# One loader operation per slot of two attention steps, in place of a whole weight in one slot

## Chip, core and metric

The kernel runs on one core of a Trainium2 chip. The metric is the device time of one execution in microseconds (us); the median of three runs of the kernel before is 1209.4 us (1208.53 to 1209.43).

## What is computed

Attention with a learned position bias over 4 batches, 8 heads, 576 positions and 64 columns, then two feed-forward layers on its 2304 x 512 result. Cut to what matters:

```python
scores = scale * q @ k.T + bias          # (4, 8, 576, 576)
attn = softmax(scores); x = attn @ v     # -> x of 2304 x 512
h = x @ w_in;  x = (h * clip(h + 3, 0, 6) / 6) @ w_out
x = (sigmoid(x @ w_gate) * (x @ w_val)) @ w_out2
```

## The kernel before

Three stages follow each other on one core: the bias (to about 61 us of the profile), the attention (61 to 345 us) and the feed-forward layers (the rest). The change touches the attention.

**Steps and slots.** Two heads (a pair) of one batch are 9 steps: 8 steps of 128 query rows of one head, and a ninth for the 64 rows left of both. There are 16 such pairs `n`, so 144 steps, and line 525 walks them in 76 slots of two steps. One slot gives TensorE the scores of its two steps (L262, into a ring of two PSUM tiles `s`), VectorE the sum with the bias and the row minimum (`u`, L266), ScalarE the exponential with its row sum (L282), and for the slot before it the transposes of the probabilities (L320, L328, L335) through a ring of three PSUM tiles `tr`, which ScalarE and VectorE copy out (L310, L312). The products with `v` (L352, L355) collect in one PSUM tile `av`, read by L359. Row sums become reciprocals in L288 and L289, which ScalarE spreads (L293) for a transpose (L299). Since two pairs are 18 steps, nine slots are the period of this work; slots 0, 9, 18, 27, ... begin one.

**Preparation of the next pair.** ScalarE rounds `q` (L230) and GpSimd does the rest of it for `q` and `k` (L234, L238): operations of over 1 us, in rows of several.

**The loader.** Weights come as float32 and are split into a high and a low part for TensorE. For one weight tile that is one DMA on SP's queue (L127, ring of two `raw`), one ScalarE operation (L133), four VectorE operations (L134, L141, L143, L145), one ScalarE rounding into the weight's `slot` (L151) and one GpSimd subtraction (L152). Ten weights are loaded in the attention: line 533 calls `whole()` in slots 12, 18, 24, ... 66. In the last slots line 537 (`tick`, slots 70 and 73) starts the next weights.

**What sets the order.** A scheduler places the instructions of all engines ahead of time, by data and buffers and by the order in which the code is written; on the chip each engine runs its list in that order. `tc.issue_after(x)` keeps the instructions that are traced under it, on the engine of `x` alone, behind `x`.

Of the kernel before, what the change touches and what calls it, by code (L numbers as in the profile page):

```python
# [14 lines left out]
ALU = mybir.AluOpType  # L15
# [28 lines left out]
NPRE = 10  # L44
EVERY = 6
# [50 lines left out]
def block_kernel(ctx: ExitStack, tc: tile.TileContext, q, k, v, mlp, w_in, w_out, w_gate, w_val, w_out2, dist_d,  # L96
                 rows_d, out):
    nc = tc.nc
# [13 lines left out]
    class Loader:  # L112
# [20 lines left out]
                nc.scalar.activation(z, self.raw[i][:, :, 1].bitcast(F32), AF.Abs)  # L133
                nc.vector.tensor_scalar(out=z, in0=z, scalar1=2.0**-15, scalar2=None, op0=ALU.max)  # L134

        def assemble(self, i):
            if i not in self.z:
                return
            raw, z = self.raw.pop(i), self.z[i]
            zi = z.bitcast(I32)  # L140
            nc.vector.tensor_scalar(out=zi, in0=zi, scalar1=3, scalar2=0x3FFFFFF8, op0=ALU.logical_shift_left,  # L141
                                    op1=ALU.bitwise_and)
            nc.vector.scalar_tensor_tensor(out=zi, in0=raw[:, :, 1], scalar=-0x40000000, in1=zi,  # L143
                                           op0=ALU.bitwise_and, op1=ALU.bitwise_or)
            nc.vector.scalar_tensor_tensor(out=zi, in0=raw[:, :, 0], scalar=29, in1=zi,  # L145
                                           op0=ALU.logical_shift_right, op1=ALU.bitwise_or)

        def split(self, i, eng=nc.vector):
            if i in self.z:
# [2 lines left out]
                eng.tensor_tensor(out=slot[:, 1], in0=z, in1=slot[:, 0].bitcast(F32), op=ALU.subtract)  # L152
                self.done = i + 1

        def whole(self):
            i = self.n
            for stage in (self.dma, self.magnitude, self.assemble):
                stage(i)
            self.split(i, nc.gpsimd)
            self.n += 1  # L160

        def tick(self):
            i = self.n
# [11 lines left out]
    def ring(name):  # L175

        if name == "z":
            return stg.tile([P, 512], F32, name="z", bufs=4)
        return stg.tile([P, 2, 512], F32, name="raw", bufs=2)

    load = Loader([w[f] for f in range(NF) for w in (w_in, w_out)]
                  + [w[e] for e in range(NE) for w in (w_gate, w_val, w_out2)])
# [66 lines left out]
    pts, us, avs, last_u = {}, {}, {}, [None]  # L249
# [113 lines left out]
    last_v = [None]  # L363
# [3 lines left out]
    for n in range(NU):  # L367
        i = (NSTEP * n + 5) // 2 + 2
# [8 lines left out]
    def slot_of_two(i):  # L377

        for t in steps(i):
            scores(t)  # L380
            n, s = seq[t]
            p, b = divmod(n, B)
            if s == 0:
                last_v[0] = load_v(n)
            if b == B - 1 and p + 1 < NPAIR and (s % 2 == 1 or s == 8):
                load_bias(p + 1, s // 2)
        for n, a, g in AV.get(i, ()):
            av(n, a, g)
            if g == 4:
                av_out(n, a)  # L390
        for t in steps(i):
            expo(t)
        for t in steps(i - 1):
            n, s = seq[t]
            if s in (5, 8):
                invert(n, s // 6 * 3, s // 6 * 2 + 3)
        for t in steps(i - 2):
            n, s = seq[t]
            if s in (5, 8):
                turn_inv(n, s // 6 * 3, s // 6 * 2 + 3)  # L400
        for t in steps(i - 1):
            trans(t)
            n, s = seq[t]
            if s in REM:
                trans_rem(n, REM[s])
        for t in steps(i):
            if t in PREP:
                n, h = PREP[t]
                prep(n, h)
            for k, (n, h) in PREP.items():  # L410
                if h == 1 and n + 1 < NU and t == k + 3:
                    load_qk(n + 1)
# [6 lines left out]
    with ExitStack():  # L419
# [24 lines left out]
        for r in (slice(NEAR, ND), slice(0, NEAR)):  # L444
# [3 lines left out]
                                op1=ALU.mult)  # L448
# [7 lines left out]
        for ct in range(4):  # L456
# [3 lines left out]
                                    op0=ALU.mult)  # L460
# [15 lines left out]
        for G in range(S // 16):  # L476
            hid = [hids[(4 * G + ct) % 12] for ct in range(4)]
            for ct in range(4):
# [4 lines left out]
                else:  # L483
                    nc.vector.tensor_scalar(out=hid[ct], in0=src, scalar1=bpsi[:, 1, qd : qd + 1], scalar2=None,  # L484
                                            op0=ALU.max)
# [14 lines left out]
        def split_x(x):  # L500
            for c in range(4):
                nc.scalar.copy(XH[:, c], x[c])
                nc.vector.tensor_tensor(out=XL[:, c], in0=x[c], in1=XH[:, c].bitcast(F32), op=ALU.subtract)

        def project(slot, ps=None):
            ps = mp.tile([P, 512], F32, name="h", bufs=4) if ps is None else ps
            for c in range(4):
                wh = slot[:, 0, P * c : P * c + P]
                wl = slot[:, 1, P * c : P * c + P]
                nc.tensor.matmul(ps[:, 0:TW], wh, XH[:, c], start=(c == 0), stop=False)  # L510
                nc.tensor.matmul(ps[:, 0:TW], wl, XH[:, c], start=False, stop=False)  # L511
                nc.tensor.matmul(ps[:, 0:TW], wh, XL[:, c], start=False, stop=(c == 3))  # L512
            return ps[:, 0:TW]

        def hardswish(g, ph):
            nc.scalar.activation(g, ph, AF.Relu, bias=half, scale=1.0 / 6.0)  # L516
            nc.vector.scalar_tensor_tensor(out=g, in0=g, scalar=1.0, in1=ph, op0=ALU.min, op1=ALU.mult)  # L517
            return g
# [5 lines left out]
        for i in range(NSLOT):  # L524
            slot_of_two(i)
            if i == NS // 2:
                w = keep.tile([P, 8 * TW], F32R, name="early").rearrange("p (r c t) -> p r c t", r=2, c=4)
                XH, XL = w[:, 0], w[:, 1]
                split_x([x[:, 0:TW] for x in x1])
            if i in (NS // 2 + 1, NS // 2 + 2):  # L530
                f = len(begun)
                begun[f] = hardswish(ring("z")[:, 0:TW], project(slots[2 * f], pp.tile([P, 2, 512], F32, name="s")[:, 0]))
            if i % EVERY == 0 and i > 10 and load.n < NPRE:
                with tc.issue_after(last_v[0].ins):
                    load.whole()
            if i in PRIME:
                load.tick()

# [156 lines left out]
```

## Time and profile before

| | |
|---|---|
| median of three runs | 1209.4 us |
| profiled execution, its own time | 1207.13 us |
| its span in the trace | 1205.4 us |
| TensorE / VectorE / ScalarE / GpSimd busy | 1187.5 / 682.1 / 574.2 / 133.2 us |
| attention | about 61 to 345 us |

All numbers of the trace belong to the profiled execution; 1.7 us of its time lie around the span. A row of the timeline gives the start, the duration, the engine, the line of the kernel, the operation and its tiles; in square brackets stands idle time ahead of it and who ended it. Matmul ends are modelled, so the distance of two starts says more than a duration. One L352 of the code is two rows of the trace.

### The profile page before, as it was taken

To read this page: it belongs to the slowest core of one execution; us is meant where nothing else is said; L and a number is where in the kernel's file an instruction comes from. 1 tells how busy PE (TensorE), PEld (TensorE's weight loads), DVE (VectorE), ACT (ScalarE), POOL (GpSimd) and SP (SyncE) were. 2 spreads that over 40 slices of the span, in tenths; PEclk is the share of its full clock that TensorE was granted. 3 is DMA by queue.
4 is the path that set the end of the run, shared out by engine and by line. 5 is a ranking of instruction groups with operands and counts; after the bars stand their busy time and mean duration, and the time that the engine had idled before them with its cause. 6 is when DMAs were issued, how large, how long until landed. Compare 5 with 4: busy or idle time off the path is not lost.

```text
span 1205.4 us, 18764 instructions
## 1 busy us (share of the span) xinstructions
PE 1187.5 (99%) x7302; PEld 1057.4 (88%) x7302; DVE 682.1 (57%) x1464; ACT 574.2 (48%) x1224; POOL 133.2 (11%) x108
## 2 busy tenths in 40 slices
PE   8989999999999999999999999999999999999998
PEld 3467777777789999999999999999999999999998
DVE  8967887778876555645565545564431544222332
ACT  7978877877854444434344434333321332221221
POOL 0055545544200000000000000000000000000000
PEclk9999999999999999999999999999999999999999
DMA  6643635353211232212222223322210121101000
GB/s 210 244 141 105 186 100 178 110 164 108 76 53 67 92 105 80 79 62 80 74 69 82 92 88 114 122 80 79 64 58 1 62 79 53 53 1 53 27 27 27
DMA packets 36152, 106.76 MB, mean 89 GB/s; under 512 B 3936, under 2 KB 10336, under 8 KB 36064
## 3 DMA queue, kind: packets, MB, share of 16 engines
q1 hardware_dynamic: 36064, 105.57, 26.9%
q8 instruction: 57, 0.93, 0.3%
q14 instruction: 31, 0.25, 0.1%
HBM read 80.78 MB, written 24.77 MB: 88 GB/s over the span
## 4 chain that ended last, share of the span: by engine, by line
PE 87%; DVE 6%; ACT 3%; DMA 2%; issue 1%; POOL 0%; SPq 0%; DVEq 0%; ACTq 0%
PE o L574 16%; PE h L512 13%; PE h L510 13%; PE h L511 13%; PE o L631 12%; PE s L262 6%; PE av L352 5%; PE tr L320 4%; PE s L489 1%; PE av L355 1%; DVE u L266 1%; DVE x L484 1%; DVE z L143 1%; ACT p L282 1%; PE tr L299 1%
## 5 line engine op out<-in xcount | busy, mean ns | idle before, releaser
L510 PE MATMUL h<-early,slot 128*128 128x384 f32 x952 | 318.9, 335 | 0.0
L512 PE MATMUL h<-early,slot 128*128 128x384 f32 x952 | 318.8, 335 | 0.0
L511 PE MATMUL h<-early,slot 128*128 128x384 f32 x952 | 318.5, 335 | 0.0
L510 PEld LDWEIGHTS h<-early,slot 128*128 128x128 f32 x952 | 178.8, 188 | 2.6
L511 PEld LDWEIGHTS h<-early,slot 128*128 128x128 f32 x952 | 178.7, 188 | 2.5
L512 PEld LDWEIGHTS h<-early,slot 128*128 128x128 f32 x952 | 178.7, 188 | 0.1
L551 ACT CAST gh<-g 128x384 fp32r<-128x384 f32 x166 | 85.0, 512 | 162.4 <-DVE g L646 119.8
L574 PE MATMUL o<-gh,slot 128*128 128x384 f32 x768 | 156.9, 336 | 3.0 <-ACT raw L310 1.8
L646 DVE TENSOR_TENSOR g<-g,h 128x384 f32<-128x384 f32 x72 | 39.8, 553 | 183.1 <-PE h L512 183.1
L574 PEld LDWEIGHTS o<-gh,slot 128*128 128x128 f32 x768 | 134.2, 188 | 6.9 <-ACT raw L310 4.4
L552 DVE TENSOR_TENSOR gl<-g,gh 128x384 fp32r<-128x384 f32 x166 | 92.2, 558 | 79.1 <-ACT gh L551 77.0
L516 ACT ACTIVATE g<-h,half 128x384 f32<-128x384 f32 x94 | 54.5, 580 | 131.1 <-PE h L512 127.5
L262 PE MATMUL s<-k,q 128*128 128x288 f32 x640 | 112.2, 310 | 2.5 <-POOL k L234 1.2
L645 ACT ACTIVATE g<-h 128x384 f32<-128x384 f32 x72 | 35.4, 492 | 165.0 <-PE h L512 165.0
L282 ACT ACTIVATE p<-u,stat 128x576 f32<-128x576 f32 x128 | 98.7, 773 | 28.9 <-DVE stat L266 28.5
L631 PE MATMUL o<-slot,gh 128*128 128x512 f32 x432 | 111.9, 393 | 0.0
L266 DVE CUSTOM_DVE_ANT_0 u<-s,bias 128x576 f32<-128x576 f32 x128 | 93.5, 753 | 24.9 <-PE s L262 24.3
L517 DVE SCALAR_TENSOR_TENSOR g<-g,h 128x384 f32<-128x384 f32 x94 | 51.8, 552 | 95.2 <-ACT g L516 95.1
L262 PEld LDWEIGHTS s<-k,q 128*128 128x128 f32 x640 | 89.0, 189 | 5.9 <-POOL k L234 1.7
L631 PEld LDWEIGHTS o<-slot,gh 128*128 128x128 f32 x432 | 80.1, 188 | 13.6 <-issue 0.2
L574 PE MATMUL o<-gl,slot 128*128 128x384 f32 x384 | 88.5, 334 | 0.0
L352 PE MATMUL av<-ptm,vn 128*64 128x288 f32 x512 | 78.9, 419 | 1.2 <-DVE x L359 0.7
(99 smaller groups left out, 1494.0 us busy)
## 6 DMA issues: line engine op xcount, KB each, us to landing
raw<-in_part_dram SPq DMA_DIRECT2D x68, 512.0 KB, 3.5
nbias<-p SPq DMA_DIRECT2D x18, 576.0 KB, 3.2
early<-in_part_dram SPq DMA_DIRECT2D x32, 288.0 KB, 4.3
bias<-nbias SPq DMA_DIRECT2D x16, 576.0 KB, 6.0
take<-x SPq DMA_DIRECT2D x12, 768.0 KB, 4.1
vn<-in_part_dram SPq DMA_DIRECT2D x16, 320.0 KB, 3.1
early<-in_part_dram SPq DMA_DIRECT2D x16, 304.0 KB, 3.8
part<-raw SPq DMA_DIRECT2D x12, 384.0 KB, 2.6
```

Source lines behind the costliest of these rows:

```text
L262: nc.tensor.matmul(ps[:, a, 0:HS], Q[:, q0 : q0 + P], K[:, r, h, HS * a : HS * a + HS], start=(i == 0), stop=(i == len(mm) - 1))
L266: last_u[0] = nc.vector.tensor_tensor_reduce(out=halves(u), in0=ps[:, :, 0:HS], in1=halves(bt), op0=ALU.add, op1=ALU.min, scale=-0.125, sc ...
L282: nc.scalar.activation(probs(t), us.pop(t), AF.Exp, bias=low[n % 2][:, s : s + 1], scale=-1.0, accum_out=sums[n % 3][:, s : s + 1])
L352: nc.tensor.matmul(ps[64 * h : 64 * h + 64, 0:HS], vt[:, 4 * h + g], ptm[:, h, g, cols], start=(g == 0), stop=False)
L510: nc.tensor.matmul(ps[:, 0:TW], wh, XH[:, c], start=(c == 0), stop=False)
L511: nc.tensor.matmul(ps[:, 0:TW], wl, XH[:, c], start=False, stop=False)
L512: nc.tensor.matmul(ps[:, 0:TW], wh, XL[:, c], start=False, stop=(c == 3))
L516: nc.scalar.activation(g, ph, AF.Relu, bias=half, scale=1.0 / 6.0)
L551: nc.scalar.copy(gh, g)
L552: last_g[0] = nc.vector.tensor_tensor(out=gl, in0=g, in1=gh.bitcast(F32), op=ALU.subtract)
L574: nc.tensor.matmul(os[c][:, 0:TW], sl[:, r, P * c : P * c + P], x, start=(first and r == 0 and x is gh), stop=(last and x is gl))
L631: nc.tensor.matmul(os[i], x[:, P * i : P * i + P], sl[:, r], start=(first and x is gh and r == 0), stop=(end and x is gl))
```

## The change

`whole()` becomes `step(k)`: slot `i` from 6 on does operation `i % 6` of the current weight. 0 is the DMA, 1 is L133 and L134, 2 to 4 are the other three VectorE operations one by one, and 5 is the ScalarE rounding with the GpSimd subtraction. A second `issue_after` keeps the VectorE operation of a slot behind the last `u` of that slot. The first weight starts in slot 6 and the tenth is done in slot 65. No instruction is added or taken away; each engine has the same ones, in another order.

```diff
-        def assemble(self, i):
+        def assemble(self, i, parts=(0, 1, 2)):
...
+            if 0 in parts:
+                nc.vector.tensor_scalar(out=zi, in0=zi, scalar1=3, scalar2=0x3FFFFFF8, op0=ALU.logical_shift_left,
...
-        def whole(self):
+        def step(self, k):
+
             i = self.n
-            for stage in (self.dma, self.magnitude, self.assemble):
-                stage(i)
-            self.split(i, nc.gpsimd)
-            self.n += 1
+            if k == 0:
+                self.dma(i)
+            elif k == 1:
+                self.magnitude(i)
+            elif k < 5:
+                self.assemble(i, (k - 2,))
+            else:
+                self.split(i, nc.gpsimd)
+                self.n += 1
...
-            if i % EVERY == 0 and i > 10 and load.n < NPRE:
-                with tc.issue_after(last_v[0].ins):
-                    load.whole()
+            if i >= EVERY and load.n < NPRE:
+                with tc.issue_after(last_v[0].ins), tc.issue_after(last_u[0].ins):
+                    load.step(i % EVERY)
```

Behind the changed functions the lines of the new kernel are 10 higher: its L276 is L266, its L298 is L288, its L142, L145 and L148 are L141, L143 and L145. The text keeps the old numbers. Three places show how the lists of the engines change; the short read of the accumulator behind each `u` is left out.

VectorE from the last `u` of slot 23 to the first of slot 25, before (`z` and `raw` are the loader's tiles):

```order
L266 ISA u,stat<-s,bias_104 128x576
L134 TENSOR_SCALAR z<-z 128x512
L359 TENSOR_TENSOR x_64<-av,inv 128x288
L312 COPY ptm<-tr 128x4x64
L141 TENSOR_SCALAR z<-z 128x512
L312 COPY ptr<-tr 64x64
L143 SCALAR_TENSOR_TENSOR z<-raw,z 128x512
L312 COPY ptm<-tr 128x4x128
```

and after:

```order
L276 ISA u,stat<-s,bias_104 128x576
L369 TENSOR_TENSOR x_64<-av,inv 128x288
L322 COPY ptm<-tr 128x4x64
L322 COPY ptr<-tr 64x64
L322 COPY ptm<-tr 128x4x128
```

Three loader operations are gone from this slot.

VectorE at the end of a pair, from the first `u` of slot 26 on (the one that reads `bias_m` is the ninth step), before:

```order
L359 TENSOR_TENSOR x_64<-av,inv 128x288
L288 TENSOR_SCALAR stat<-stat 128x6
L289 RECIPROCAL stat<-stat 128x6
L312 COPY ptm<-tr 128x4x128
L266 ISA u,stat<-s,bias_106 128x576
L266 ISA u,stat<-s,bias_m 128x576
L312 COPY ptm<-tr 128x4x128
L266 ISA u,stat<-s,bias_103 128x576
```

and after:

```order
L369 TENSOR_TENSOR x_64<-av,inv 128x288
L134 TENSOR_SCALAR z<-z 128x512
L322 COPY ptm<-tr 128x4x128
L276 ISA u,stat<-s,bias_106 128x576
L298 TENSOR_SCALAR stat<-stat 128x6
L276 ISA u,stat<-s,bias_m 128x576
L299 RECIPROCAL stat<-stat 128x6
L142 TENSOR_SCALAR z<-z 128x512
L322 COPY ptm<-tr 128x4x128
L276 ISA u,stat<-s,bias_103 128x576
```

L288 (new L298) has moved from ahead of both `u` to between them, in slots 17, 26, 35, 44, 53 and 62 alike; in slot 62 a fourth loader operation, L145, stands right behind it, from the weight that line 537 starts. In the slot that follows, 28, the list reads L288, L143, L289 where it read L288, L289, and so also in slots 10, 46 and 64.

TensorE from slot 27 on (`s` scores, `av` products with v), before:

```order
L262 MATMUL s<-k_110,q_108 128x288 x8
L352 MATMUL av<-ptm,vn 64x288 x6
L299 MATMUL tr<-ident,spread 128x128 x3
L320 MATMUL tr<-ident,p 128x128 x4
L328 MATMUL tr<-ident,pm_113 128x64 x4
L262 MATMUL s<-k_110,q_108 128x288 x4
L328 MATMUL tr<-ident,pm_113 128x64 x4
```

and after:

```order
L272 MATMUL s<-k_110,q_108 128x288 x8
L362 MATMUL av<-ptm,vn 64x288
L272 MATMUL s<-k_110,q_108 128x288
L309 MATMUL tr<-ident,spread 128x128 x3
L272 MATMUL s<-k_110,q_108 128x288
L362 MATMUL av<-ptm,vn 64x288 x5
L330 MATMUL tr<-ident,p 128x128 x4
L338 MATMUL tr<-ident,pm_113 128x64 x4
```

A score matmul of the next slot now stands ahead of five of the six products with `v` (slots 27 and 45). On ScalarE the rounding of `q` (L230) has moved there from behind the exponentials of the pair's last two steps to ahead of them, and the copy of `tr` that stood between them stands behind both and behind L293.

## Rows read from the trace of the kernel before

**Rows 1.** The page: busy time and instructions by engine; granted TensorE clock in tenths.

```profile
PE 1187.5 (99%) x7302; PEld 1057.4 (88%) x7302; DVE 682.1 (57%) x1464; ACT 574.2 (48%) x1224; POOL 133.2 (11%) x108
...
PEclk9999999999999999999999999999999999999999
```

**Rows 2.** Windows of nine slots: length, then busy PE, PEld, DVE, ACT, POOL.

```profile
127.15:162.59 35.44, 34.52 (x257) 26.24 (x256) 29.95 (x74) 28.40 (x75) 18.66 (x15) 1.00 0.49 152
162.59:196.78 34.19, 34.19 (x258) 26.23 (x256) 25.86 (x70) 27.67 (x73) 17.21 (x14) 1.00 0.42 120
196.78:232.23 35.45, 34.50 (x258) 26.23 (x256) 29.87 (x74) 28.39 (x75) 18.57 (x15) 1.00 0.47 143
232.23:266.41 34.18, 34.18 (x257) 26.22 (x256) 25.85 (x70) 27.66 (x73) 17.20 (x14) 1.00 0.43 119
```

**Rows 3.** Timeline, VectorE: loader operations of slots 24 and 38.

```profile
149.97 1.19 DVE L134 TENSOR_SCALAR z<-z 128x512 f32<-128x512 f32 x1
...
151.78 0.94 DVE L141 TENSOR_SCALAR z<-z 128x512 int32<-128x512 int32 x1
...
204.62 1.92 DVE L143 SCALAR_TENSOR_TENSOR z<-raw,z 128x512 int32<-128x512 int32 x1
```

**Rows 4.** Timeline, GpSimd, near slots 24 and 35 to 38.

```profile
147.95 2.93 POOL L238 TENSOR_TENSOR q<-early,q 64x640 fp32r<-64x640 f32 x2
150.96 1.48 POOL L238 TENSOR_TENSOR k<-early,k 128x576 fp32r<-128x576 f32 x1
...
195.73 2.25 POOL L234 TENSOR_TENSOR k<-early,one 128x576 fp32r<-128x576 f32 x2 [8.19 <-PE s L262]
197.94 2.79 POOL L238 TENSOR_TENSOR k<-early,k 128x576 fp32r<-128x576 f32 x2
200.80 1.55 POOL L238 TENSOR_TENSOR q<-early,q 64x640 fp32r<-64x640 f32 x1
204.57 1.42 POOL L238 TENSOR_TENSOR q<-early,q 64x576 fp32r<-64x576 f32 x1 [2.22 <-ACT q L230]
```

**Rows 5.** Timeline, TensorE: its waits in slots 24 and 25; slots 36 and 37.

```profile
151.91 0.66 PE L320 MATMUL tr<-ident,p 128*128 128x128 f32 x4 [0.21 <-DVE ptm L312]
...
157.04 0.66 PE L320 MATMUL tr<-ident,p 128*128 128x128 f32 x4 [0.48 <-ACT inv L310]
...
196.78 1.30 PE L262 MATMUL s<-k,q 128*128 128x288 f32 x8
198.00 1.68 PE L352 MATMUL av<-ptm,vn 128*64 128x288 f32 x12
...
201.64 0.46 PE L328 MATMUL tr<-ident,pm 64*128 64x64 f32 x4
```

**Rows 6.** Timeline, VectorE, slots 35 to 37: a pair's end and the next pair's start.

```profile
193.96 0.16 DVE L288 TENSOR_SCALAR stat<-stat 128x6 f32<-128x6 f32 x1
...
194.49 0.69 DVE L312 COPY ptm<-tr 128x512 f32<-128x512 f32 x1
...
195.77 0.08 DVE L266 DVE_READ_ACCUMULATOR2_ANT stat<- 128x1 f32 x1
196.08 0.76 DVE L266 CUSTOM_DVE_ANT_0 u<-s,bias_m 128x576 f32<-128x576 f32 x1 [0.22 <-PE s L262]
...
197.68 0.76 DVE L266 CUSTOM_DVE_ANT_0 u<-s,bias 128x576 f32<-128x576 f32 x1
...
199.04 0.33 DVE L288 TENSOR_SCALAR stat<-stat 128x3 f32<-128x3 f32 x1
...
201.75 0.76 DVE L266 CUSTOM_DVE_ANT_0 u<-s,bias 128x576 f32<-128x576 f32 x1 [2.16 <-PE s L262]
```

**Rows 7.** Timeline, ScalarE: in the bias stage, and in slots 35 to 37.

```profile
30.63 0.78 ACT L482 ACTIVATE x<-x,early 128x576 f32<-128x576 f32 x1 [1.31 <-PE s L489]
...
196.67 0.56 ACT L310 COPY ptm<-tr 128x512 f32<-128x512 f32 x1
...
200.59 0.48 ACT L310 COPY inv<-tr 128x384 f32<-128x384 f32 x1
```

More of the change, by code (lines that the diff above doesn't have):

```diff
@@ L134, in magnitude @@
                 nc.vector.tensor_scalar(out=z, in0=z, scalar1=2.0**-15, scalar2=None, op0=ALU.max)
-        def assemble(self, i):
+        def assemble(self, i, parts=(0, 1, 2)):
             if i not in self.z:
                 return
-            raw, z = self.raw.pop(i), self.z[i]
+            raw, z = self.raw[i], self.z[i]
             zi = z.bitcast(I32)
[L141 to L146, printed above, removed]
+            if 0 in parts:
+                nc.vector.tensor_scalar(out=zi, in0=zi, scalar1=3, scalar2=0x3FFFFFF8, op0=ALU.logical_shift_left,
+                                        op1=ALU.bitwise_and)
+            if 1 in parts:
+                nc.vector.scalar_tensor_tensor(out=zi, in0=raw[:, :, 1], scalar=-0x40000000, in1=zi,
+                                               op0=ALU.bitwise_and, op1=ALU.bitwise_or)
+            if 2 in parts:
+                nc.vector.scalar_tensor_tensor(out=zi, in0=raw[:, :, 0], scalar=29, in1=zi,
+                                               op0=ALU.logical_shift_right, op1=ALU.bitwise_or)
+                self.raw.pop(i)
         def split(self, i, eng=nc.vector):
```

## The prediction

> **What bounds the kernel now.** I read the busy times first: TensorE has 1187.5 of 1205.4 us and the granted clock is full in every slice [rows 1], so the change pays by what it does to TensorE's waits, and the clock is no term. No instruction is added or removed, so only the order in the attention counts. There I read windows of nine slots, the period of the attention's work [rows 2]. They come in two lengths, 34.18 to 34.19 and 35.44 to 35.45 us. The short ones hold one load (slots 30 and 48), the long ones two (18 and 24, 36 and 42). In a short one TensorE is busy to the end, 34.19 of 34.19: this I take as the pace that no reordering beats. A long one has 0.95 less busy time than length.
>
> Then I ask which operation makes a long window long. In slot 24 the loader's L134 takes 1.19 us and its L141 0.94 [rows 3]; shortly behind each a GpSimd operation that was running has ended: the second of two L238 at 150.88 and the next at 152.44 [rows 4]; the loader operation is done some 0.28 us after that. L143 in slot 38 took 1.92 and was done 0.55 after GpSimd's L238 of 204.57. L288 at 199.04 waited in the same way, 0.33 in place of 0.16 [rows 6]. So these VectorE operations stand still until the running GpSimd operation ends. TensorE's waits right behind them are 0.21 on VectorE's copy and 0.48 on ScalarE's [rows 5].
>
> The Trainium skill (SBUF — State Buffer, section "Who interferes with whom") says that the second port pair of VectorE is GpSimd's too, is held for a whole instruction and goes to whoever issues first, and that tensor_scalar and operations with two SBUF inputs ask for it. The trace shows the VectorE half of it, with the times above; no row here shows GpSimd standing behind VectorE.
>
> **What is removed.** Loads in slots 18, 36 and 54 with their partners in 24, 42 and 60 make three long windows, each 35.44 - 34.18 = 1.26 us over the short one. Loads in 30 and 48 cost nothing, since their windows are short, and I take the same for 12 and 66. At best the change gives back 3 x 1.26 = 3.8 us.
>
> **What is added: four terms.** Times are those of slots 35 to 37 [rows 4 to 7], which stand for every pair's end.
>
> (a) A pair's end, six times. L288 ran at 193.96, when GpSimd was idle (8.19 us before 195.73). Now it comes behind the slot's first `u`, at 195.77 + 0.08 = 195.85, and GpSimd has started two L234 at 195.73 that end at about 196.86 and 197.98. So L288 stands until 196.9, and the ninth step's `u` starts there and not at 196.08. It frees the score tile which the second step of the next slot needs: its first matmul comes at about 197.3 (eight from 196.78 on, the next kind at 198.00), the tile is free at 196.9 + 0.76 = 197.7, so TensorE is 0.4 late. In slots 18, 36 and 54 nothing of the loader follows, and part comes back later, because the new order lets TensorE work where it waited ahead of L328 at 201.64. I take 0.3 each, 0.9 in all; bounds 0 and 1.2.
>
> (b) Slots 27 and 45. On top of (a), L141 follows L289 and stands until the second L234 ends: done 197.98 + 0.28 = 198.3; the copy of 0.69 ends at 199.0, and the next `u`, at 197.68 before, starts then and is done at 199.7. TensorE has one product with `v` (0.27) behind its late scores and then a score matmul that needs this `u`: it idles from about 198.5 to 199.7. ScalarE's copy for the other five products, at 196.67 before, comes behind the ninth step's exponential and L293, at about the same 199.6, so no other order of TensorE would save it. 0.4 + 1.2, less the 0.2 that TensorE lost ahead of 198.00 anyway, is 1.4. A part may come back at L328 (1.05 left); if L143 in slot 28, behind L288, misses the gap between two GpSimd operations and stands behind the L238 of 200.80, 0.8 is added to that, 1.85. I take the middle, 1.45, twice: 2.9; bounds 2.1 and 3.7.
>
> (c) Slot 62. L145 of the weight that line 537 starts stands behind L288 ahead of the ninth step's `u`. At 196.9 GpSimd's second L234 runs to 197.98, and as an operation of L143's form it is done 0.55 later, 198.5; that `u` ends at 199.3, and TensorE's second step waits from 197.3: 2.0. L143 in slot 64 can add 1.3. At least it costs what (b) may, 1.05, at most 3.3; I take 2.7, nearer the upper end because L288, L145, L141 and L143 follow each other there into one row of GpSimd operations.
>
> (d) Slots 9 and 10, the first weight. Slot 8 keeps its order, but L141 meets GpSimd (done 198.3), the two `u` end 1.3 us late, L288 stands until the two L238 end at 200.73, and L143 either slips in (L289 done at 201.6) or stands until 200.80 + 1.55 + 0.55 = 202.9 (L289 at 203.1). ScalarE's copy at 200.59 needs it through L293, and TensorE's L328 at 201.64 needs the copy: 0.75 or 2.2 late. I take 1.5, between the two, since the rows do not tell who wins that gap.
>
> **At nothing.** The other loader operations of the new order: a nine-slot window leaves VectorE 34.19 - 25.86 = 8.3 us idle, and in slots 13 to 16, 20 to 24 and 30 to 34 they meet either an idle GpSimd or stand ahead of an L288 that waits for the same GpSimd operation anyway. Without that cover each would cost up to L143's 1.92. The first weight's DMA and L133 move into the bias stage; L133, some 0.7, falls into ScalarE's idle 1.31 ahead of 30.63 [rows 7]; without that cover 0.7, which I add to the upper end. On SP each raw load of weights 1 to 9 stands where that of the weight before stood, so nothing of `q`, `k`, `v` waits longer there.
>
> **Sum.** Added 0.9 + 2.9 + 2.7 + 1.5 = 8.0, removed 3.8: 4.2 us slower. Bounds: 0 + 2.1 + 1.05 + 0.75 - 3.8 = 0.1 and 1.2 + 3.7 + 3.3 + 2.2 + 0.7 - 3.8 = 7.3. The profiled execution took 1207.1 us, 2.3 less than the median; on it the sum gives 1211.3, on the median 1209.4 + 4.2 = 1213.6, and I say 1213.5.
>
> **Rivals.** *It does what it is meant to* (faster): the loader's work hides in every slot, L288 between the two `u` meets no GpSimd operation, and all of 3.8 comes back: 1205.6. The point that decides is 0.12 us wide: L288 at 195.85 against GpSimd's 195.73. Both follow TensorE's scores of the same step, so I see nothing that would open it; for it speaks only that `u` two microseconds late in slot 20 cost little in the old kernel. 0.12.
>
> *The losses cancel the gain*: TensorE takes back part of each delay, L143 slips in each time, and the terms are at their low ends, 3.9 against 3.8: 1209.5. It decides itself in slots 28 and 64, where the trace of before has nothing of the loader. 0.32.
>
> *L143 wins its gap*: VectorE's L143 starts in the gap between two GpSimd operations in slots 10, 28 and 46, and the next GpSimd operation waits for it. Then (b) is at its 2.1 and (d) at its 0.75, with (a) and (c) as taken: 0.9 + 2.1 + 2.7 + 0.75 - 3.8 = 2.65 over, 1212.05. This is about half of my forecast's 0.56, which it moves by 1.5 and not to another sign. The Trainium skill's rule (SBUF — State Buffer, section "Who interferes with whom") that the first to issue holds the pair speaks for it.
>
> *The change doesn't do what it says*: the tie holds VectorE alone, and the lists of ScalarE, GpSimd and TensorE are free. The order shows that the VectorE operations do come one per slot, so this is left only for ScalarE's L133 and L151, which stand next to each other ahead of two exponentials in slots 23, 41 and 59. I count it in the upper end.
>
> **How the numbers follow.** The forecast, slower by 2.5 to 7.3, has 0.56; the cancelled case 0.32; the hidden one 0.12. A measurement of this kernel can tell about 0.2% (2.4 us) from no change, so faster means under 1207.0 and slower over 1211.8: 0.12, 0.32, 0.56. The likeliest case's own range is 1211.8 to 1216.7. The range to hold 8 in 10 leaves out the hidden case and a little above the sum's upper end: 1207.0 to 1216.7.
>
> **What would show it.** In the profile of the changed kernel, the nine-slot windows from slots 18, 36 and 54 should be about 34.5 us and no longer 35.4, those from 27 and 45 about 35.6, the one from 63 over 36, the one from 9 about 35.7. L288 at each pair's end should take 1 us or more, and TensorE should wait for the `u` behind it. If L288 there takes 0.16, (a) to (c) fall and with them the sign. If it does take 1 us but the window from slot 27 stays near 34.2, then TensorE's list absorbs what I booked as loss, and the time is that of the cancelled case or below.

## The result and the profile after

The changed kernel takes 1215.75 us (median of 4 runs, 1215.52 to 1216.55) against 1208.99 us for the kernel before, so the medians are 6.8 us apart. The recorded ratio is 1.0066 (95% interval 1.0053 to 1.0078), which is not the quotient of the medians and would be 8 us; either way it is slower, clear of noise. The forecast was slower, at 1213.5. The profiled execution of before lies 1.9 us under its median and that of the changed kernel at its median, so the two traces stand 8.6 us apart (spans 1214.0 and 1205.4). The terms below are those of the traces. Lines of the changed kernel keep its own numbers: L298, L142, L145, L148 are what the prediction calls L288, L141, L143, L145.

The page's busy line, to be held against [rows 1]: no instruction more, 5.6 us more of TensorE, and 5.7 more of GpSimd and 6.7 of VectorE for the same work, so operations of these engines stood longer.

```profile
PE 1193.1 (98%) x7302; PEld 1058.9 (87%) x7302; DVE 688.8 (57%) x1464; ACT 575.8 (47%) x1224; POOL 138.9 (11%) x108
```

The windows of nine slots (from the first score matmul of slots 9, 18, 27, 36, 45 and 54; length, then busy PE, PEld, DVE, ACT, POOL), to be held against [rows 2]:

```profile
92.64:127.47 34.83, 34.44 (x257) 26.19 (x256) 28.75 (x71) 27.93 (x74) 19.80 (x15) 1.00 0.47 137
127.47:163.19 35.72, 35.39 (x257) 26.38 (x256) 27.82 (x69) 27.89 (x74) 18.51 (x14) 1.00 0.47 144
163.19:199.68 36.49, 35.45 (x257) 26.43 (x256) 30.25 (x73) 28.65 (x76) 18.80 (x15) 1.00 0.40 120
199.68:235.40 35.72, 35.24 (x257) 26.39 (x256) 27.73 (x69) 27.90 (x74) 18.51 (x14) 1.00 0.44 135
235.40:271.91 36.51, 35.47 (x257) 26.45 (x256) 30.27 (x73) 28.66 (x76) 18.79 (x15) 1.00 0.40 118
271.91:307.65 35.74, 35.22 (x257) 26.39 (x256) 29.11 (x72) 28.38 (x75) 18.53 (x14) 1.00 0.46 141
```

No window is short any more. Against the old short window, 34.18, they are 0.65, 1.54, 2.31, 1.54, 2.33 and 1.56 over. The last slots (63 to 70) took 33.78 in place of 31.44, 2.3 more. That is 12.2 us lost, and 3.8 of it was lost before: 8.4, nearly all of the 8.6 between the traces.

To find the places I took the starts of all slots from the timeline (a slot starts with its first score matmul) and held each slot against the same one of a short window (slots 27 to 35 of before: 4.15, 4.41, 3.91, 3.35, 4.54, 3.27, 4.05, 3.92, 2.57 us). The loss stands in three places: the two or three slots behind a pair's end, slots 15, 33 and 51 (4.62 in place of 4.05), and slots 24 and 25, 42 and 43, 60 and 61 (0.6 for each two).

The first place, on VectorE, slots 34 to 37 (timeline, the lines that [rows 6] has of before):

```profile
196.86 0.68 DVE L148 SCALAR_TENSOR_TENSOR z<-raw,z 128x512 int32<-128x512 int32 x1
...
198.73 0.85 DVE L298 TENSOR_SCALAR stat<-stat 128x6 f32<-128x6 f32 x1
199.49 0.74 DVE L276 CUSTOM_DVE_ANT_0 u<-s,bias_m 128x576 f32<-128x576 f32 x1
...
200.17 0.18 DVE L299 RECIPROCAL stat<-stat 128x6 f32<-128x6 f32 x1
...
202.19 0.97 DVE L298 TENSOR_SCALAR stat<-stat 128x3 f32<-128x3 f32 x1
```

and on GpSimd in the same stretch, against [rows 4]:

```profile
198.27 1.28 POOL L156 TENSOR_TENSOR slot<-z,slot 128x512 fp32r<-128x512 f32 x1 [8.15 <-ACT slot L155]
199.51 2.25 POOL L244 TENSOR_TENSOR k<-early,one 128x576 fp32r<-128x576 f32 x2
201.72 2.79 POOL L248 TENSOR_TENSOR k<-early,k 128x576 fp32r<-128x576 f32 x2
```

L298 between the two `u` does stand, 0.85 in place of 0.16. But what it stands behind is L156, the loader's own subtraction, which I had not placed there (it ends at 199.55, L298 at 199.58); L156 then pushes GpSimd's row back, so that the next L298 takes 0.97 in place of 0.33.

### The profile page after: what moved, and what is told of

Its sections match the earlier page's. It is cut to its first block, busy times and chain, and to the rows that moved or that the text cites. A ratio compares the mean times of both kernels' runs of the same rounds, so it can differ in the third digit from the quotient of the medians.

```text
span 1214.0 us, 18776 instructions
## 1 busy us (share of the span) xinstructions
PE 1193.1 (98%) x7302; PEld 1058.9 (87%) x7302; DVE 688.8 (57%) x1464; ACT 575.8 (47%) x1224; POOL 138.9 (11%) x108
## 4 chain that ended last, share of the span: by engine, by line
PE 86%; DVE 6%; ACT 5%; DMA 2%; issue 1%; POOL 0%; SPq 0%; DVEq 0%; ACTq 0%; POOLq 0%
PE o L584 16%; PE h L522 13%; PE h L520 13%; PE h L521 13%; PE o L641 12%; PE s L272 5%; PE av L362 5%; PE tr L330 4%; PE s L499 2%; ACT p L292 2%; PE av L365 1%; DVE u L276 1%; DVE stat L298 1%; ACT p L477 1%; DMA part<-raw 1%
## 5 line engine op out<-in xcount | busy, mean ns | idle before, releaser
L276 DVE CUSTOM_DVE_ANT_0 u<-s,bias 128x576 f32<-128x576 f32 x128 | 93.1, 752 | 19.3 <-PE s L272 18.6
L362 PE MATMUL av<-ptm,vn 128*64 128x288 f32 x512 | 83.7, 419 | 0.5 <-DVE ptm L322 0.5
```

The lines of the kernel that those rows point to most:

```text
L276: last_u[0] = nc.vector.tensor_tensor_reduce(out=halves(u), in0=ps[:, :, 0:HS], in1=halves(bt), op0=ALU.add, op1=ALU.min, scale=-0.125, sc ...
L362: nc.tensor.matmul(ps[64 * h : 64 * h + 64, 0:HS], vt[:, 4 * h + g], ptm[:, h, g, cols], start=(g == 0), stop=False)
```

## The experiments

Theory A says that VectorE's operations stand until a GpSimd operation ends; theory B, that the loader's operations and the moved ones cost by their places in the lists alone. C and D came up on the way, in the expectations of e5 and e9.

### e1 and e2: without most of GpSimd's work

```diff
         high(on[0], Q[0:D], qt)
-        high(on[1], K[:, 0], kt)
...
+        wq, wk = (32, 32) if n > 1 else (qt.shape[-1], S)
+        high(on[1], K[:, 0, 0:wk], kt[:, 0:wk])
+        low(on[2], Q[D:P, 0:wq], qt[:, 0:wq], Q[0:D, 0:wq])
...
```

> The kernel before, in which GpSimd's preparation operations of every pair from the third on do 32 columns in place of 576 or 640 (so the products of these pairs are of old data); the lists of TensorE, VectorE and ScalarE stay word for word those of before. Theory A (VectorE's operations stand until a running GpSimd operation ends): all nine-slot windows become as long as the short ones, 34.18 us, so the three long ones give back 1.26 each and the kernel takes 1209.0 - 3.8 = 1205.2 us. Theory B (the loader's operations cost by their own time at their places in the lists): the long windows stay near 35.4 and the time within 1 us of 1209.0.

> The changed kernel with the same cut of GpSimd's preparation; its lists are nearly those of the changed kernel. Theory A: the windows from slots 27 and 45 (36.5 us) fall to 34.2 to 34.6, those from 18, 36 and 54 (35.72) to about 34.8, since there ScalarE's rounding and L133 ahead of two exponentials stay and cost 0.6 without GpSimd; the kernel takes 1207 to 1208 us. Theory B: the windows stay within 0.3 us of 36.5 and 35.72, and the kernel takes 1214 to 1216 us.

e1 takes 1202.25 us (ratio 0.9942, 0.9928 to 0.9957), e2 1207.34 (0.9988, 0.9979 to 0.9997). GpSimd's rows shrink to 32 columns, so both kernels work on old data and are for timing alone. Windows of e1 from slots 18 and 27, then of e2 from 18, 27, 36 and 45:

```profile
127.38:161.49 34.11, 34.11 (x258) 26.26 (x256) 26.89 (x74) 28.58 (x75) 5.45 (x14) 1.00 0.48 142
161.49:195.67 34.18, 34.18 (x257) 26.23 (x255) 24.92 (x70) 27.57 (x73) 4.18 (x13) 1.00 0.48 129
```

```profile
127.40:162.67 35.27, 35.11 (x258) 26.37 (x256) 25.19 (x72) 27.71 (x74) 5.49 (x14) 1.00 0.47 139
162.67:197.62 34.95, 34.95 (x257) 26.41 (x256) 26.32 (x74) 28.45 (x76) 5.38 (x14) 1.00 0.47 128
197.62:232.54 34.92, 34.92 (x257) 26.37 (x256) 25.22 (x72) 27.72 (x74) 5.51 (x14) 1.00 0.47 136
232.54:267.51 34.97, 34.97 (x258) 26.43 (x256) 26.33 (x74) 28.44 (x76) 5.39 (x14) 1.00 0.47 124
```

For the kernel before, theory A holds within 0.1 us: the long window is as short as the short one, and TensorE, VectorE and ScalarE have the same lists. (The time fell 3 us below the expected 1205.2: 1.2 us were gained behind slot 71, and the trace that the 3.8 were read from stands 1.9 under the median.) For the changed kernel neither theory holds alone: the time is what theory A expected, but the windows are 0.1 to 0.5 us over its figures. The loss in slots 33 and 42 to 43 is gone (4.02, and 4.05 with 3.87), but about 0.8 us per window stays in the first two slots: slots 36 and 37 take 4.14 and 5.17, where short windows have 4.15 and 4.41. (Slot 24 alone keeps another 0.3.) From the start of slot 0 to that of slot 71, the traces take 268.9 us (e1), 274.4 (e2), 272.7 (before) and 281.2 (changed). So the lists alone cost 5.5, and GpSimd adds 3.8 to the old ones and 6.8 to the new, 3.0 net. (The lists of e2 are those of the changed kernel up to slot 60; from there some entries stand elsewhere, so the share of the last slots, 1.1 of the 5.5, is less sure.) From slot 71 to the end, e1 and e2 take 870.9 and 870.4, the two full kernels 872.1 and 872.6, though nothing was edited there; why is open.

The 0.8 was found by reading ScalarE's and TensorE's rows of e2 beside those of e1. ScalarE in slot 36, first of e1 (the slot starts at 195.67), then of e2 (197.62); the two kernels have their own line numbers, one higher than in the text:

```profile
197.57 0.77 ACT L283 ACTIVATE p<-u,stat 128x576 f32<-128x576 f32 x1
```

```profile
198.80 0.50 ACT L304 COPY spread<-stat 128x384 f32<-128x384 f32 x1
...
199.99 0.78 ACT L293 ACTIVATE p<-u,stat 128x576 f32<-128x576 f32 x1
```

In e2 VectorE's L298 between the two `u` does not stand for more than some hundredths (its line is L299 there):

```profile
196.67 0.22 DVE L299 TENSOR_SCALAR stat<-stat 128x6 f32<-128x6 f32 x1
```

With L299 of the changed kernel behind the ninth step's `u`, ScalarE's spread L303 (0.5 us) falls between the ninth exponential and the next pair's first one. That exponential then starts 2.37 us into the slot and not 1.90, the second spread, the copies behind it and the transposes L338 follow 0.5 late, and TensorE stands ahead of L345 and behind it. This is theory C. The busy column does not show it: TensorE reads as busy to the end in e2's windows too, 34.92 of 34.92, and they are 0.74 longer than the short ones with the same matmuls.

### e3: without the tie behind u

```diff
-                with tc.issue_after(last_v[0].ins), tc.issue_after(last_u[0].ins):
+                with tc.issue_after(last_v[0].ins):
```

> The changed kernel without its second tie, the one behind the slot's last u; the loader's code still does one operation per slot. The lists then stand nearly as before, with two to four loader operations in one slot, and L298 ahead of both u at a pair's end. If the loss comes with the tie (theories A and B alike): the windows from 27 and 45 return to 34.2 to 34.3, those from 18, 36 and 54 stay near 35.4, since slots 23 and 24 read as before, and the kernel takes 1208 to 1210 us. If writing one operation per slot costs by itself (the DMA and L133 of a weight a slot or more ahead): over 1213 us.

1209.72 us, ratio 1.0007 (0.9998 to 1.0017): no difference that can be told. Windows from slots 27 and 36:

```profile
163.88:198.07 34.19, 34.19 (x258) 26.22 (x256) 25.86 (x70) 27.67 (x73) 17.23 (x14) 1.00 0.43 119
198.07:233.25 35.18, 34.44 (x258) 26.22 (x256) 28.96 (x74) 28.21 (x75) 18.58 (x15) 1.00 0.48 145
```

Writing one operation per slot changes next to nothing, because the scheduler pulls the operations together again, up to two slots ahead. The tie alone spreads them, and most of the loss comes with it, though not that of the last slots (63 to 65 are 1.2 over here too). The window from 18 was 36.21, a miss of 0.8: L142, L145 and L148 fell together into slot 20 there.

### e4 and e5: L298 and L299 ahead of both u

```diff
+        end = i > 8 and i % 9 == 8
+        if end:
+            invert(seq[2 * i - 2][0], 0, 3)
         for t in steps(i):
-            scores(t)
+            with tc.issue_after(last_r[0].ins) if end else ExitStack():
+                scores(t)
```

> The changed kernel with L298 and L299 of a pair's end put back ahead of both u (the reciprocal is called ahead of the scores, and the two u are tied behind it); the loader's operations stay one per slot behind u. My prediction's theory (L298 between the two u is what costs in terms a to c): the windows from 27 and 45 fall from 36.5 to about 35.3, those from 18, 36 and 54 from 35.72 to about 35.2, and the kernel gains 4 to 5 us, to about 1211. The rival (the loader's operations L142, L145 and L148 themselves, wherever L298 stands, and ScalarE's rounding in slots 16 to 43): less than 1.5 us gained, over 1214 us.

> As e4_inverse_ahead_of_u, and ScalarE's rounding of q (L240) that e4 had drawn ahead of the pair's-end exponentials is tied behind the ninth step's exponential, where it stands in the kernel before. The loader is that of the changed kernel. Theory C (of the changed kernel's loss, about 0.8 us of each window from slots 18 to 54 comes from L298's place: the spread L303 falls behind the ninth step's exponential and everything of ScalarE after it is 0.5 late): the losses of e4 in slots 18, 27, 36, 45 and 54 (4.92 in place of 4.14) vanish, the windows from 18, 36 and 54 come to about 34.8, those from 27 and 45 to about 34.9, and the kernel takes 1208.5 to 1210 us. The rival (the loader's operations cost as much wherever L298 stands): windows stay at 35.6 to 35.8 and the kernel at 1212 to 1213 us.

e4 takes 1212.54 us (1.0028, 1.0018 to 1.0037) and e5 1212.02 (1.0029, 1.0019 to 1.0039). Windows from slots 27 and 36, of e4 and then of e5:

```profile
164.02:199.64 35.62, 35.21 (x258) 26.35 (x256) 28.47 (x73) 28.47 (x75) 18.49 (x15) 1.00 0.41 120
199.64:235.41 35.77, 35.27 (x257) 26.36 (x256) 27.72 (x72) 28.03 (x75) 18.60 (x14) 1.00 0.46 138
```

```profile
163.10:198.12 35.02, 34.63 (x258) 26.48 (x256) 28.71 (x73) 28.08 (x74) 18.54 (x15) 1.00 0.42 121
198.12:233.25 35.13, 34.62 (x257) 26.67 (x256) 27.66 (x72) 28.01 (x74) 18.58 (x14) 1.00 0.45 139
```

e4 was no clean undoing: the moved call drew ScalarE's L240 ahead of the pair's-end exponentials, and slot 36 took 4.92, 0.77 too long. With L240 held back too most of that is gone (4.49), and e5 takes 1.47 off the windows from 27 and 45 and 0.6 off those from 18, 36 and 54. From slot 0 to 71 its trace is 5.3 us shorter than that of the changed kernel (the medians are 3.7 apart; the profiled execution is the fastest of e5's nine). The windows, 35.1 and 35.0, are nearer to C's 34.8 and 34.9 than to the rival's 35.6 to 35.8, but the median is the rival's, 1212 to 1213, and not C's 1208.5 to 1210. So the placing of L298 costs what these windows gained; that ScalarE's order is the path of it rests on e2, since e5 also takes L298 out of GpSimd's way. What stays in slots 36 to 38 is 0.3: the second L298 still took 1.23 us there, behind the GpSimd row that L156 pushed back.

### e6: L142 one slot later, e9: L148 one slot earlier

The edit of e6, and then that of e9:

```diff
-                    load.step(i % EVERY)
+                    if i % 18 == 15:
+                        load.step(2)
+                    if i % 18 != 14:
+                        load.step(i % EVERY)
```

```diff
-                    load.step(i % EVERY)
+                    if i % 18 != 4:
+                        load.step(i % EVERY)
+                    if i % 18 == 3:
+                        load.step(4)
```

> The changed kernel with L142 of slots 14, 32 and 50 moved one slot later, ahead of L145, where GpSimd is idle; all else of the lists stays but three pairs of ScalarE and TensorE instructions. Theory A (L142 there stands until GpSimd's L248 ends, 1.21 us, and the copy of ptm behind it comes late): slots 15, 33 and 51 fall from 4.62 to 4.03 to 4.1 us, three times 0.55, and the kernel takes about 1214.1 us. Theory B (any loader operation more ahead of those copies costs its own time): slots 15, 33 and 51 stay over 4.4, and the kernel within 0.6 us of 1215.75.

> The changed kernel with L148 of slots 22, 40 and 58 moved into the slot before, where GpSimd is idle; TensorE's list stays as it is, ScalarE's L155 moves up with it and L133 stays ahead of the exponentials in slots 23, 41 and 59. Theory D (L148 in slot 40 holds GpSimd's next operation up, 1.86 in place of 1.41 us, and L298, which stands behind that operation, is released 0.45 later; all of slots 41 to 43 follows): slots 42 and 43 fall from 4.07 and 4.50 to 4.05 and 3.92, the windows from 18, 36 and 54 from 35.72 to about 35.15, and the kernel takes about 1214.0 us. Rival (ScalarE's L133 and L155 in a row ahead of the exponentials, which my prediction named): with L133 still there at least half of the loss stays, slot 43 over 4.2, and the kernel within 1 us of 1215.75.

In the changed kernel, VectorE and GpSimd in slot 32 and TensorE's wait in slot 33, the second place of loss:

```profile
187.65 1.21 DVE L142 TENSOR_SCALAR z<-z 128x512 int32<-128x512 int32 x1
```

```profile
185.64 2.93 POOL L248 TENSOR_TENSOR q<-early,q 64x640 fp32r<-64x640 f32 x2
```

```profile
189.61 0.66 PE L330 MATMUL tr<-ident,p 128*128 128x128 f32 x4 [0.39 <-DVE ptm L322]
```

e6 takes this away: slots 15, 33 and 51 are 4.07, 4.05 and 4.06. The kernel takes 1215.01 us (1.0053, 1.0039 to 1.0066), 0.7 less and not the 1.7 that the three slots give, and four runs of each hardly tell 0.7 from nothing. In its trace slots 18, 36 and 54 were 0.05 to 0.08 longer and slot 4 was 0.4 longer.

The third place, slot 40 of the changed kernel, VectorE and then GpSimd:

```profile
219.16 1.14 DVE L148 SCALAR_TENSOR_TENSOR z<-raw,z 128x512 int32<-128x512 int32 x1
220.22 1.37 DVE L298 TENSOR_SCALAR stat<-stat 128x3 f32<-128x3 f32 x1
...
222.30 0.75 DVE L276 CUSTOM_DVE_ANT_0 u<-s,bias 128x576 f32<-128x576 f32 x1
```

```profile
217.50 2.25 POOL L244 TENSOR_TENSOR k<-early,one 128x576 fp32r<-128x576 f32 x2 [5.87 <-PE s L272]
219.71 1.86 POOL L248 TENSOR_TENSOR k<-early,k 128x576 fp32r<-128x576 f32 x1
221.65 2.93 POOL L248 TENSOR_TENSOR q<-early,q 64x640 fp32r<-64x640 f32 x2
```

L148 stands until the second L244 is done, then runs ahead of L248, and L248 takes 1.86 where the same one takes 1.42 in e9. L298 stands behind that L248, and the `u` behind it starts 5.84 us behind slot 40's start (216.46), in a short window of before 5.35 (183.78 less 178.43). In e9, slots 42 and 43 come to 4.05 and 4.13, two thirds of the loss off. What stays, 0.2, is open. ScalarE's L133 kept its place, but so it did in e2, where slots 42 and 43 lost nothing; and in e9 L156 has come between two of GpSimd's L248. No run moved either alone.

e9 took 1213.40 us (1.0040, 1.0027 to 1.0054), more off than expected, and its windows from slots 18, 27 and 36 say why:

```profile
127.72:163.16 35.44, 35.28 (x258) 26.41 (x256) 27.18 (x72) 27.91 (x74) 18.07 (x14) 1.00 0.48 145
163.16:198.74 35.58, 35.17 (x258) 26.39 (x256) 28.74 (x72) 28.46 (x76) 18.90 (x15) 1.00 0.40 121
198.74:234.10 35.36, 35.26 (x257) 26.42 (x256) 27.18 (x72) 27.89 (x74) 18.05 (x14) 1.00 0.46 139
```

The window from 27 lost 0.9 us though nothing was edited in it. Slot 26 there, VectorE and GpSimd of the changed kernel, and then of e9:

```profile
162.19 1.13 DVE L298 TENSOR_SCALAR stat<-stat 128x6 f32<-128x6 f32 x1
```

```profile
162.14 2.25 POOL L244 TENSOR_TENSOR k<-early,one 128x576 fp32r<-128x576 f32 x2 [7.04 <-PE s L272]
```

```profile
162.15 0.17 DVE L298 TENSOR_SCALAR stat<-stat 128x6 f32<-128x6 f32 x1
```

```profile
162.16 2.47 POOL L244 TENSOR_TENSOR k<-early,one 128x576 fp32r<-128x576 f32 x2 [7.12 <-PE s L272]
```

L298 came 0.05 us behind L244 in the one and 0.01 ahead of it in the other, and there the two L244 took 0.22 longer. Slots 27 and 28 together take 10.32 us in the changed kernel, 9.38 in e9 and 8.56 in a short window: with L298 free, 0.8 of the loss is still there, as in e2.

### e7 and e8: whole weights, at one phase or tied

Both start from the kernel before; e8 adds the second tie to its loads, and e7 moves them:

```diff
-            if i % EVERY == 0 and i > 10 and load.n < NPRE:
+            if i in (3, 4, 5, 12, 21, 30, 39, 48, 57, 66):
```

> The kernel before, whole weight at once, with the loads in slots 3, 4, 5, 12, 21, 30, 39, 48, 57 and 66 in place of 12, 18, 24, ... 66: from slot 9 on one load in each nine slots, at the place where those of slots 12, 30 and 48 cost nothing. Theory A: every nine-slot window reads as the short ones, 34.2 us, so 3 x 1.26 = 3.8 us come back, 1205.2 us, less what the loads in slots 3 to 5 cost beside TensorE's wait of 9.4 us for the bias (0 to 1 us). Rival: the loads in slots 3 to 5 delay the bias tables or the first pairs by more than they save, over 1208 us; or the old long windows came from their number of loads and not their place, which one load in each window must then share out as 34.8.

> The kernel before, a whole weight in one slot in slots 12, 18, ... 66, with the second tie behind the slot's last u alone. If the tie is what costs (e3 without it came back to the kernel before): slots 24, 31 and 42 now have loader operations between u and the copies of the transposes, each long window stays at 35.4 to 36 and the short ones grow by 0.3 to 1 us; 1210 to 1213 us. If tie and spreading cost only together: 1208 to 1210 us.

e7 takes 1208.25 us (0.9994, 0.9984 to 1.0003). Its windows from 18 and 27:

```profile
131.97:166.14 34.17, 34.17 (x257) 26.21 (x256) 25.75 (x70) 27.69 (x73) 18.26 (x14) 1.00 0.46 139
166.14:200.33 34.19, 34.19 (x258) 26.23 (x256) 25.86 (x70) 27.70 (x73) 17.25 (x14) 1.00 0.42 120
```

Theory A and its rival both came true in part: one load in each window at that place is free, and the three early loads gave the gain back. Slot 9 starts at 97.79 and not at 92.99. The waits of slots 4 and 5 (us in total, times, longest) show TensorE standing for GpSimd's L234, and that for the transfer of `q` and `k`, behind which SP issued one of the extra `raw` loads. The transfer landed up to 5.6 us after its issue, in the kernel before 4.3:

```profile
PE s L262 <- POOL k L234: 2.1, 1, 2.1
...
POOL k L234 <- DMA early<-in_part_dram: 2.6, 1, 2.6
```

These are a part of the 4.8 us. TensorE stood 1.2 for an L234 in that stretch of the kernel before too, and what makes up the rest is open.

e8 takes 1213.49 us (1.0039, 1.0026 to 1.0052). Windows from 18 and 27:

```profile
127.83:162.32 34.49, 34.27 (x257) 26.25 (x256) 28.27 (x71) 27.80 (x72) 18.52 (x15) 1.00 0.50 157
162.32:199.01 36.69, 35.89 (x258) 26.61 (x256) 27.52 (x72) 28.80 (x76) 16.92 (x13) 1.00 0.36 106
```

The long window became nearly short, against my expectation: behind `u` the load of slot 24 costs nothing (slots 24 and 25 take 4.06 and 3.93). The window from 27 grew by 2.5, all in slots 27 and 28, since here L288 and L289 have gone behind both `u` of slot 26. Once more it is the pair's end that pays for the tie.

### e10, e11, e12: versions from what was learned

e10 ties only the loads of slots 24, 42 and 60, with L288, L289 and L230 kept in place as in e5; e11 is one line:

```diff
-            if i % EVERY == 0 and i > 10 and load.n < NPRE:
+            if i in (12, 18, 21, 30, 36, 39, 48, 54, 57, 66):
```

e12 is the changed kernel with the edits of e5, e6 and e9 together.

> The kernel before with whole weights in slots 12, 21, 30, 39, 48, 57 and 66, where e7 showed them free, and three more in slots 24, 42 and 60, these tied behind u as in e8, where slots 24 and 25 lost nothing, with L288 and L289 of the next pair's end kept ahead of both u and L230 behind the ninth exponential as in e5. Theory: windows from 9, 27 and 45 at 34.2 to 34.6 (their loads come 0.3 to 0.6 of a slot later behind the pair's end), those from 18, 36 and 54 at 34.2 to 34.3, in all 2 to 3.5 us off: 1205.5 to 1207 us. Rival: the tie costs at the pair's end as in e8, windows from 27 and 45 over 35.4, and the kernel over 1209.

> The kernel before with whole weights in slots 12, 18, 21, 30, 36, 39, 48, 54, 57 and 66: the three long windows keep the load of slots 18, 36 and 54 (0.29 in slot 20 of before) and have their second in slot 21, 39, 57 and not in 24, 42, 60 (0.98 in slots 24 and 25 of before). Theory A: the windows from 18, 36 and 54 fall from 35.44 to 34.5 to 34.9, and the kernel by 1.6 to 2.8 us, to 1206 to 1207.2. Rival: the second load, pushed back by the first, has its last operation in slot 22 ahead of u, where GpSimd is busy, and costs as much there: 1208.5 to 1209.

> The changed kernel with all three mends: L298 and L299 ahead of both u and L240 behind the ninth exponential (e5), L142 of slots 14, 32 and 50 one slot later (e6), L148 of slots 22, 40 and 58 one slot earlier (e9). If the losses add (0.57 in slots 15, 33, 51; 0.6 in slots 42 and 43; the rest at the pair's end): windows from 27 and 45 at about 34.45, from 18, 36 and 54 at about 34.5, the last slots still 1.4 over the kernel before; 207 us for the six windows against 208.9, and 1208 to 1209 us. If they do not add (one loss hides another): windows stay over 34.8 and the kernel over 1210.

e11 beats both kernels: 1205.71 us (1203.46 to 1206.21) against 1208.62 for the kernel before, ratio 0.9970 (0.9958 to 0.9981). e10 does too: 1205.69, 0.9980 (0.9971 to 0.9989), though its windows from 27 and 45 missed their 34.6. e12 takes 1208.59, ratio 0.9999 (0.9990 to 1.0008). Windows from 18 and 27 of e10, of e11 and of e12:

```profile
127.10:161.27 34.17, 34.17 (x257) 26.21 (x256) 27.55 (x74) 28.53 (x73) 19.53 (x15) 1.00 0.51 159
161.27:196.23 34.96, 34.96 (x258) 26.42 (x256) 24.98 (x70) 28.26 (x75) 17.19 (x14) 1.00 0.41 123
```

```profile
127.02:161.48 34.46, 34.23 (x258) 26.23 (x256) 28.25 (x74) 28.94 (x75) 19.35 (x15) 1.00 0.50 150
161.48:195.64 34.16, 34.16 (x258) 26.20 (x256) 25.87 (x70) 27.66 (x73) 17.23 (x14) 1.00 0.42 119
```

```profile
129.01:163.71 34.70, 34.64 (x257) 26.64 (x256) 26.20 (x72) 27.91 (x74) 18.22 (x14) 1.00 0.52 161
163.71:198.18 34.47, 34.47 (x257) 26.54 (x256) 28.04 (x72) 28.02 (x74) 18.41 (x15) 1.00 0.40 120
```

In e11 only the 0.3 of the load in slots 18, 36 and 54 is left. In e12 the mended losses add as expected: the spread loader itself is then better than the old one from slot 9 to 62 (207.3 us for the six windows against 208.9), though the windows from 18, 36 and 54 are 0.2 over the expected 34.5. The last slots, 1.4 over in e5 with the same placing and 1.6 over here, give it back. In the trace of e12 slots 4 and 5 took 2.3 us longer too, and why is open; its profiled execution lies 1.1 us over its median.

## Why the prediction was right and where not

The direction and the place were right: slower, above all by L298 at the pair's end. The mechanism was right in part. Contention with GpSimd was to make the whole loss there, but e2, nearly without it, still loses 0.8 us at each of these places: of the 2.85 and 3.5 us of terms (a) and (b) below about 2.4 and 1.6 come from the lists alone. The size was 4.2 over where 6.8 was measured. Term by term, from the trace:

| term | predicted | in the trace |
|---|---|---|
| removed: the three long windows | -3.8 | -3.8 |
| (a) slots 18, 36, 54 and the two behind each | 0.9 (0 to 1.2) | 2.85 |
| (b) slots 27 to 29, 45 to 47 | 2.9 (2.1 to 3.7) | 3.5 |
| (c) slots 63 on | 2.7 (1.05 to 3.3) | 2.3 |
| (d) slots 9 and 10, with the slot behind | 1.5 (0.75 to 2.2) | 0.1 |
| "at nothing": slots 15, 33, 51; 24, 42, 60 | 0 | 3.5 |

- The step that failed is **At nothing**, taken as 0 and measured at 3.5 us. I let loader operations meet GpSimd wherever an L288 stood behind the same GpSimd operation anyway. That took GpSimd's times as given. Slot 40 shows that they are not: a VectorE operation that runs first makes the next GpSimd operation later, and the L298 behind it with that. In slot 32 there was no such L298 at all, and the copies of the transposes stood behind L142 (e6). The doubt about L133 and L151 side by side in slots 23, 41 and 59, which I had put into the upper end, can be at most the third of it that e9 left; in e2 it cost nothing in slots 42 and 43.
- **Term (a)** was mis-sized by a factor of three, beyond its upper bound. The ninth step's `u` came 0.5 late against the slot's start, less than the 0.8 I had worked out, but I counted only the score tile that waits for it. The longer path goes from L299 over ScalarE's spread to the next pair's exponentials (e2), and it is there even when L298 does not stand. "Part comes back later" did not happen; more was lost in slot 37 than in slot 36. Nor had I placed the GpSimd subtraction of the loader's last step, which stands ahead of the pair's first L244 in these slots.
- **Term (d)** fell away: in slot 9, L142 found GpSimd idle (0.42) and L145 a gap (0.68). The premise that slots 35 to 37 stand for every pair's end failed here, and the trace of before showed it: GpSimd's row of slot 9 waits for a transfer and starts 0.49 behind the slot's start (92.99), where that of slot 36 starts 1.05 ahead of it.

```profile
93.48 2.25 POOL L234 TENSOR_TENSOR k<-early,one 128x576 fp32r<-128x576 f32 x2 [5.15 <-DMA early<-in_part_dram]
```

- **Terms (b) and (c)** lie within their bounds, but by other pieces, so their size is luck. In (b), L145 in slot 28 did win its gap at 0.68, the rival *L143 wins its gap* (GpSimd's next operation took 1.80 for it), which should have put (b) at 2.1; it came to 3.5, of which about 1.6 stands in e2 too, theory C's part. In (c), L148 in slot 62 took 0.68 and did not stand, so the ninth step's `u` was 1.3 late and not 2.4; 0.98 was lost in slot 63 and 1.20 in slot 65, and what makes the latter is open.
- The rival *it does what it is meant to* named a point that decides, L288 against GpSimd, 0.12 us wide. e9 crossed it unplanned in slots 26 and 44 and got 0.9 us per pair's end, not the whole 1.8, since theory C's part stays.
- What would show it: the windows from 18, 36 and 54 were to be 34.5 and are 35.7; from 27 and 45, 35.6 and are 36.5; from 9, 35.7 and is 34.83. The last slots, where the window was to be over 36, have no ninth start to measure it by. L288 at the pair's end was to take 1 us or more and takes 0.85 to 1.13. The sign "if L288 there takes 0.16, (a) to (c) fall and with them the sign" was wrong: in e2 it takes 0.22, and e2 is still 5.1 us slower than e1.
- That the time fell inside the stated range, 1207.0 to 1216.7, is luck in part. (a) and **At nothing** came out 5.5 over together and (d) 1.4 under, and the 8.4 between the traces lies over the sum's upper bound of 7.3.

## What to carry to other kernels

Where each engine runs a list that was ordered ahead, a tie on one engine is an edit to all: look where the *other* instructions went, above all those that feed a third engine, and follow each to its last reader. Filling idle slots gained nothing by itself here; a whole weight in the one phase where the neighbour engine idles was free (e7, e11), and the same operations one per slot were not. And a shared resource has no fixed schedule to hide behind: whoever runs first moves the other.

## What the runs showed of the hardware

- The contention of VectorE and GpSimd goes both ways, and who starts first decides. L298 took 1.13 us when it came 0.05 behind L244 and 0.17 when it came 0.01 ahead. GpSimd's L248 took 1.86 in place of 1.42 behind a running L148. The Trainium skill (SBUF — State Buffer, section "Who interferes with whom") says that the order of issue decides who blocks; these rows agree.
- Not every VectorE operation stands. L299, a reciprocal of one SBUF operand, took 0.18 at 200.17 us in the middle of GpSimd's L244 (199.51 to 201.76); L298, on the same operand, took 0.85 beside L156.
- Runs of one kernel spread wider than I had allowed for: 25 runs of the kernel before gave 1206.6 to 1210.4 us, so two single traces can stand 2 us further apart than the medians.
